# The first sequence of a gated attention kernel shares its scores between groups; the token sort works in two borrowed buffers

## The chip, the cores and the metric

The kernel runs on one core of a Trainium2 chip. The metric is the device time of one execution in microseconds (us), as the median of several runs. A profiled execution also gives a trace: every instruction with its start and its length, by engine. PE is TensorE (PEld its weight loads), DVE is VectorE, ACT is ScalarE, POOL is GpSimd, and SP is the engine whose queue issues most transfers.

## The reference

Two blocks follow each other. The first is gated attention over 8 sequences of 2496 tokens, without a softmax:

```
scores = z @ z^T / S            # z: (8, 2496, 64); each sequence's scores are symmetric
attn   = max(scores, 0) ** 2
x      = u * (attn @ v)         # u, v, x: (8, 2496, 256)
```

The second sends each of the 19968 tokens to one of 8 experts, by a hash of its id, and computes `max(x_e @ w1[e], 0) @ w2[e]` with w1 of 256 x 1024 and w2 of 1024 x 256. All in fp32.

## The kernel before, in words

**Tiling.** A sequence has 20 tiles of 128 tokens (T; the last holds 64), taken in five groups of four (G, NG). For a sequence b and a group g of queries, `scores` multiplies z with z on TensorE: one matmul gives a 128 x 512 block, tile t of the keys against the 512 queries of the group, into one of six PSUM buffers. A ReLU on the way to SBUF (L209 to L212) and a square in SBUF (`square`, L215) make it the attention weight. Four such blocks make a buffer `a`, of which there are seven (NA). `attend` then multiplies the weights with v, 4 matmuls per tile of keys, and accumulates in `acc`; `gate` multiplies with u and the constant.

**Sharing.** The block of keys t and queries s is the transpose of the block of keys s and queries t. From the second sequence on (`mirrored(b)`, L171) a group computes only the blocks of its own and of later groups (`fresh`), and VectorE transposes the blocks of a later group into a buffer `m` (`turns_of`, 16 instructions of 32 partitions x 512 for a 512 x 512 block), from which that later group reads them (`lhs`). Within a group's own 512 x 512 block part is skipped and transposed as well (`skipped`, `own_turns`; `fine(g)` is true for groups 2 to 4). The first sequence computes all 20 tiles in each group, its squares are on VectorE, and its ReLUs alternate between ScalarE and VectorE. In later sequences the squares are on ScalarE, and so are the ReLUs, but for every eighth one in groups 0 and 1.

**Order.** The order of all instructions on each engine is the program's, written out by hand. The loop over the 40 groups (L589) runs, for each group, in steps of four attention matmuls: a step squares two more tiles, calls `turn_scores(1)`, which puts out transposes worth 1600 elements of budget (a transposition of 512 elements is charged 682), and calls `between()`, which puts out one piece of other work. The next group's scores are put ahead of a group's last three tiles of attention, and the gates behind those. Transposes that must be done before a buffer is used again, or before a tile is read, are put out at once by `turn_now`.

**The other work.** In the first 40 steps, two groups long, `between` takes the next piece of `places()`, the token sort on VectorE (with six count matmuls on TensorE at L420), and at every fourth step `clear_x`, 2176 KB of zeros to the rows of x in DRAM. After that it puts out scatters on POOL: slots (`enter`) and rows of x (`place_x`). The sort keeps its arrays in a pool of its own, `route`, which is closed when the sort is done; the six turned buffers `m` are made after that, at the start of the fifth group.

**Loads.** SP's queue takes, in this order: z, v and u of the first sequence; at each group u of the next (two buffers: it waits for the gates two groups back); at a sequence's first group the z and v of the next (z has one buffer, v two); and the clears. The first z comes in a layout that TensorE transposes (L158); the later ones come in 12 transfers of runs of 128 bytes (L136 and L138) and are turned by VectorE in the fifth group (`turn_z`, L154).

Of the kernel before, what the change touches and what calls it, by code (L numbers as in the profile page):

```python
# [24 lines left out]
def kernel(  # L25
# [25 lines left out]
    G = 4  # L51
# [119 lines left out]
    def mirrored(b):  # L171
        return b > 0

    def fresh(b, g):

        if not mirrored(b):
            return [*range(T)]
        return [*range((g + 1) * G, T), *group(g)]

    def summed(b, g):  # L180

        own = group(g) if mirrored(b) else ()
        return [t for t in range(TM) if t not in own] + [t for t in own if t < TM]

    def skipped(b, g, t):

        if not mirrored(b) or t // G != g:
            return 0
        return (t % G if fine(g) else t % G // 2 * 2) * P

    def fine(g):

        return g > 1
# [3 lines left out]
    def scores(b, g):  # L197

        n = sum(width(t) for t in group(g))
        for k, t in enumerate(fresh(b, g)):  # L200
            lo = skipped(b, g, t)
            h = ds((t % 2 if t % G < 2 or not mirrored(b) else 1 - t % 2) * K, K)
            ps = mm_ps.tile([P, G * P], F32, name="s_ps", tag="mm")
            nc.tensor.matmul(ps[:, lo:n], zT[b][h, ts(t, P)], zT[b][h, ds(g * G * P + lo, n - lo)], start=True, stop=True)  # L204
            if t % G == 0:
                made[b, g, t // G] = apool.tile([P, G, G * P], F32, name="a", tag="a")
                rooms.append((b, g, t // G))
            a = made[b, g, t // G][:, t % G, lo:n]
            if (k % 8 == 7 and g < 2) if mirrored(b) else k % 2:  # L209
                nc.vector.tensor_scalar_max(a, ps[:, lo:n], 0.0)  # L210
            else:
                nc.scalar.activation(a, ps[:, lo:n], AF.Relu)  # L212
            to_square.append((b, g, t))

    def square(n):  # L215
        for b, g, t in to_square[:n]:
# [6 lines left out]
            for o, x in pairs:  # L223
                if mirrored(b):
                    nc.scalar.square(o, x)  # L225
                else:
                    nc.vector.tensor_mul(o, x, x)
            if mirrored(b) and t % G == G - 1:
# [46 lines left out]
    def turn_scores(steps):  # L275

        nonlocal turned
        turned += steps * 1600
# [94 lines left out]
    def places():  # L373

        with tc.tile_pool(name="route", bufs=1) as route:
# [16 lines left out]
            ones = route.tile([P, E * C], F32)  # L392
            nc.gpsimd.memset(ones[:], 1.0)

# [4 lines left out]
            for n, cols in ((P, slice(0, TM)), (R, slice(TM, T))):  # L399
# [4 lines left out]
            mask = route.tile([P, E, C], BF16)  # L404
            nc.vector.tensor_tensor(
                mask[:], eid[:].rearrange("p b t -> p (b t)").unsqueeze(1).to_broadcast([P, E, C]),
# [6 lines left out]
            total = route.tile([P, E, C], F32)  # L413
            rank = route.tile([P, E, C], F32)
# [8 lines left out]
            upto = route.tile([P, E, C], F32)  # L423
            flat = "p e c -> p (e c)"
            nc.vector.tensor_tensor_scan(upto[:].rearrange(flat), ones[:], total[:].rearrange(flat), 0.0,
                                         op0=OP.mult, op1=OP.add)
            yield
            nc.vector.tensor_add(rank[:], rank[:], upto[:])
            yield
            nc.vector.tensor_sub(rank[:], rank[:], total[:])  # L430
# [58 lines left out]
            nc.vector.tensor_add(rank[:], rank[:], shift[:].unsqueeze(2).to_broadcast([P, E, C]))  # L489
            yield  # L490
            nc.vector.tensor_mul(rank[:], rank[:], mask[:])
            yield
            slot = route.tile([P, C], F32)
            nc.vector.tensor_reduce(slot[:], rank[:].rearrange("p e c -> p c e"), axis=AX.X, op=OP.add)
# [91 lines left out]

    scores(0, 0)
    square(EARLY)
    for n, (b, g) in enumerate(groups):  # L589
        if n + 1 < len(groups):  # L590
            load_u(*groups[n + 1])
        if g == 0 and b + 1 < B:
            load_z(b + 1)
            load_v(b + 1)
        if n == NG - 1:
            m = pool("mirror", 1)
            mirrors = [m.tile([P, G, G, P], F32, name=f"m_{k}") for k in range(NG * NG // 4)]
# [171 lines left out]
```

## Time and profile before

The median of three runs is 2685.01 us (2684.61 to 2685.49). The profiled execution took 2687.06 us, with a span of 2685.1 us from its first to its last instruction, at a mean granted TensorE clock of 0.999.

| stretch, by the start of its first score matmul (us) | length | PE busy | DVE busy | ACT busy | DMA share |
|---|---|---|---|---|---|
| sequence 0, group 0: 13.79 to 53.93 | 40.14 | 38.72 | 30.22 | 6.55 | 1.01 |
| group 1: 53.93 to 96.58 | 42.65 | 42.65 | 28.95 | 5.97 | 1.02 |
| group 2: 96.58 to 139.24 | 42.66 | 42.66 | 21.10 | 5.97 | 0.29 |
| group 3: 139.24 to 181.89 | 42.65 | 42.65 | 20.60 | 5.97 | 0.08 |
| group 4: 181.89 to 221.03 | 39.14 | 39.14 | 23.52 | 5.80 | 0.09 |
| sequence 1, group 0: 221.03 to 262.55 | 41.52 | 41.20 | 31.42 | 18.43 | 0.48 |
| group 1: 262.55 to 303.05 | 40.50 | 40.50 | 34.01 | 14.60 | 0.09 |
| group 2: 303.05 to 341.63 | 38.58 | 38.58 | 33.15 | 10.89 | 0.09 |
| group 3: 341.63 to 378.49 | 36.86 | 36.86 | 30.74 | 6.86 | 0.09 |
| group 4: 378.49 to 411.04 | 32.55 | 32.55 | 23.93 | 3.05 | 0.11 |

A row is a stretch between the first score matmuls of two groups; since a group's scores stand ahead of the last three tiles of the group before, each stretch but the very first begins with one block of scores, ends the group before, and then attends. DMA share is the mean busy share of the 16 DMA engines. The other six sequences follow (the last score matmul starts at 1519.3 us), and the experts fill the rest. A line of a timeline gives start, us, engine, line of the kernel, operation, output and input, shapes and count; what stands in brackets at its end is how long the engine was idle before it and what ended that. Instructions that overlap on one engine are merged, so a line of 20 matmuls with 20 weight loads is x40.

### The profile page before, as it was taken

The page shows a single profiled execution, that of the slowest core. Times are in us where ns is not written, and L with a number is a line of the kernel's source. Part 1 is how long each engine was busy: PE and PEld are TensorE (multiplying, and loading weights), DVE is VectorE, ACT ScalarE, POOL GpSimd, SP SyncE. Part 2 cuts the span into 40 slices and gives each one's busy share as a digit, 9 for nine tenths or more (in the row PEclk, how much of TensorE's full clock was granted, in tenths as well). Part 3 has the DMA queues.
Part 4 walks back from the last instruction along what each step waited for, and adds up shares of the span by engine and source line. Part 5 has one row for each costly group of instructions (what it writes and reads, how often), then busy time and mean ns, then how long its engine had stood idle before and what let it go on. Part 6 is the DMA issues. An engine that isn't in the chain of part 4 may idle for free. (4 is left out here: it accounts for less than half of the span.)

```text
span 2685.1 us, 33980 instructions
## 1 busy us (share of the span) xinstructions
PE 2662.1 (99%) x12650; PEld 2255.2 (84%) x12650; DVE 1357.5 (51%) x2813; ACT 567.6 (21%) x1221; POOL 494.2 (18%) x513
## 2 busy tenths in 40 slices
PE   8999999999999999999999999999999999999998
PEld 6877887888888888888878888888888888888887
DVE  6556886887878878878878811111111111111110
ACT  2013314214222233123132111111111111111111
POOL 0221222122212221222101121111111111111113
PEclk9999999999999999999999999999999999999999
DMA  9612113013103122131101287777777777777773
GB/s 295 206 31 74 32 32 89 17 32 89 31 20 87 31 46 62 29 90 32 32 16 32 62 200 188 187 188 193 195 187 190 188 187 186 194 194 192 188 189 88
DMA packets 334842, 308.93 MB, mean 115 GB/s; under 512 B 187308, under 2 KB 293693, under 8 KB 334672
## 3 DMA queue, kind: packets, MB, share of 16 engines
q1 hardware_dynamic: 309424, 264.78, 39.2%
q0 software_dynamic: 21072, 41.10, 5.2%
q8 instruction: 102, 1.67, 0.3%
q10 hardware_dynamic: 4176, 0.82, 0.2%
q14 instruction: 68, 0.56, 0.1%
HBM read 243.25 MB, written 65.70 MB: 115 GB/s over the span
## 5 line engine op out<-in xcount | busy, mean ns | idle before, releaser
L329 PE MATMUL acc<-v_sb,a 128*128 128x256 f32 x3760 | 828.7, 380 | 3.7 <-issue 2.2
L329 PEld LDWEIGHTS acc<-v_sb,a 128*128 128x128 f32 x3760 | 710.3, 190 | 112.5 <-issue 7.9
L241 DVE STREAM_TRANSPOSE m<-a 32x512 f32<-32x512 f32 (+1 forms) x1120 | 756.8, 676 | 17.1 <-issue 0.3
L683 DVE TENSOR_SCALAR hT<-h_ps 128x512 f32<-128x512 f32 x162 | 112.1, 692 | 951.0 <-PE h_ps L675 933.9
L675 PE MATMUL h_ps<-v_sb,m 128*128 128x256 f32 x2592 | 586.0, 379 | 2.2 <-issue 1.1
L688 PE MATMUL o_ps<-m,hT 128*128 128x256 f32 x2592 | 585.2, 379 | 0.0
L675 PEld LDWEIGHTS h_ps<-v_sb,m 128*128 128x128 f32 x2592 | 492.3, 190 | 70.3 <-issue 2.1
L688 PEld LDWEIGHTS o_ps<-m,hT 128*128 128x128 f32 x2592 | 492.5, 190 | 67.0
L329 PE MATMUL acc<-v_sb,m 128*128 128x256 f32 x2016 | 439.7, 379 | 0.0
L329 PEld LDWEIGHTS acc<-v_sb,m 128*128 128x128 f32 x2016 | 383.0, 190 | 52.1
L212 ACT ACTIVATE a<-s_ps 128x512 f32<-128x512 f32 (+3 forms) x442 | 205.7, 578 | 902.9 <-PE s_ps L204 902.9
L522 POOL DMA_INDIRECT x_rows<-x_sb,slot_i x160 | 157.8, 986 | 1075.4 <-DVE x_sb L338 884.8
L700 POOL DMA_INDIRECT out_dram<-o_sb,idx x158 | 153.5, 972 | 918.7 <-ACT o_sb L695 903.8
L695 ACT COPY o_sb<-o_ps 128x256 f32<-128x256 f32 x162 | 60.3, 372 | 741.4 <-PE o_ps L688 737.5
L204 PE MATMUL s_ps<-zT 64*128 64x512 f32 (+5 forms) x1040 | 211.2, 549 | 0.0
L257 DVE STREAM_TRANSPOSE a<-a 32x128 f32<-32x128 f32 (+2 forms) x896 | 201.4, 249 | 7.8
L225 ACT ACTIVATE a<-a 128x512 f32<-128x512 f32 (+3 forms) x413 | 202.1, 625 | 0.0
L204 PEld LDWEIGHTS s_ps<-zT 64*128 64x128 f32 x1040 | 123.9, 187 | 81.8 <-issue 57.2
L510 POOL DMA_INDIRECT slot_tokens<-token,addr x160 | 158.8, 993 | 159.4 <-DVE addr L504 109.1
L681 ACT ACTIVATE hT<-h_ps 128x512 f32<-128x512 f32 x162 | 96.7, 597 | 229.0 <-PE h_ps L675 218.2
L210 DVE TENSOR_SCALAR a<-s_ps 128x512 f32<-128x512 f32 (+1 forms) x78 | 51.4, 659 | 146.6 <-PE s_ps L204 145.5
L338 DVE SCALAR_TENSOR_TENSOR x_sb<-acc,u_sb 128x256 f32<-128x256 f32 x152 | 57.9, 420 | 133.7 <-PE acc L329 132.8
(80 smaller groups left out, 380.6 us busy)
## 6 DMA issues: line engine op xcount, KB each, us to landing
m<-in_moe_w_dram SPq DMA_DIRECT2D x324, 256.0 KB
m<-in_moe_w_dram SPq DMA_DIRECT2D x81, 1024.0 KB
x_rows<-zero SPq DMA_DIRECT2D x10, 2176.0 KB
v_sb<-x_rows SPq DMA_DIRECT2D x324, 64.0 KB
v_sb<-in_v_dram SPq DMA_DIRECT2D x32, 512.0 KB
u_sb<-in_u_dram SPq DMA_DIRECT2D x32, 512.0 KB
zn<-in_z_dram SPq DMA_DIRECT2D x28, 304.0 KB
v_sb<-in_v_dram SPq DMA_DIRECT2D x8, 384.0 KB
```

Source lines behind the costliest of these rows:

```text
L204: nc.tensor.matmul(ps[:, lo:n], zT[b][h, ts(t, P)], zT[b][h, ds(g * G * P + lo, n - lo)], start=True, stop=True)
L212: nc.scalar.activation(a, ps[:, lo:n], AF.Relu)
L225: nc.scalar.square(o, x)
L241: nc.vector.transpose(mirror[b, a, g][ts(c, Q)].rearrange("p t s q -> p (t s) q")[:, 0:m, ts(r, Q)], made[b, a, g][ts(r, Q)].rearrange("p ...
L257: return n * Q, lambda: nc.vector.transpose(out, in_)
L329: nc.tensor.matmul(acc[i // 2][:, i % 2, :], lhs(b, g, t, i), v_sb[b][:, t, :], start=(k == 0 and i % 2 == 0), stop=(k == TM - 1), skip_gr ...
L510: st = nc.gpsimd.indirect_dma_start(out=slot_dram[:, None], out_offset=bass.IndirectOffsetOnAxis(ap=addr[0:n, c:c + 1], axis=0), in_=token ...
L522: st = nc.gpsimd.indirect_dma_start(out=x_dram[:, :], out_offset=bass.IndirectOffsetOnAxis(ap=slot_i[0:width(c % T), c:c + 1], axis=0), in ...
L675: nc.tensor.matmul(ps[:, i, :], w1[j][:, c, ts(f + i, P)], xT[j][:, :, c, :], start=(c == 0), stop=(c == DP - 1))
L683: nc.vector.tensor_scalar_max(o, ps[:], 0.0)
L688: nc.tensor.matmul(ps[:], hT[j][:, f, ts(t, P)], w2[j][:, f, :], start=(f == 0), stop=(f == FP - 1))
L700: st = nc.gpsimd.indirect_dma_start(out=out[:], out_offset=bass.IndirectOffsetOnAxis(ap=rows, axis=0), in_=o, in_offset=None, bounds_check ...
```

## The change

- `mirrored` is gone: the first sequence shares as the others do. Its groups 0 and 1 compute their own block in full (`skipped` is 0 there, and there are no `own_turns`); groups 2 to 4 skip and transpose as elsewhere. Group 0's scores come in the order of tiles 4 to 19, 0 to 3.
- All squares are on ScalarE. The ReLUs alternate between ScalarE and VectorE only in the first group of the first sequence. There the first two squares are put out after the eleventh score.
- The six turned buffers exist from the start. One of them, `sorting`, holds `upto` and `mask` of the sort until the third group begins, and joins the others then; `total` and `rank` lie in the z buffer, taken after the first z. `ones` shrinks to 8 columns and is broadcast in the long scan.
- The next sequence's z is loaded at group 2 instead of group 0, for all sequences.
- The budget of `turn_scores` is 1300 in the first 40 steps.

```diff
@@ -168,27 +168,23 @@
 
 
 
-    def mirrored(b):
-        return b > 0
-
     def fresh(b, g):
 
-        if not mirrored(b):
-            return [*range(T)]
         return [*range((g + 1) * G, T), *group(g)]
 
     def summed(b, g):
 
-        own = group(g) if mirrored(b) else ()
+        own = group(g)
         return [t for t in range(TM) if t not in own] + [t for t in own if t < TM]
 
     def skipped(b, g, t):
 
-        if not mirrored(b) or t // G != g:
+        if t // G != g or b == 0 and not fine(g):
             return 0
         return (t % G if fine(g) else t % G // 2 * 2) * P
 
     def fine(g):
+
 
         return g > 1
 
@@ -199,18 +195,20 @@
         n = sum(width(t) for t in group(g))
         for k, t in enumerate(fresh(b, g)):
             lo = skipped(b, g, t)
-            h = ds((t % 2 if t % G < 2 or not mirrored(b) else 1 - t % 2) * K, K)
+            h = ds((t % 2 if t % G < 2 else 1 - t % 2) * K, K)
             ps = mm_ps.tile([P, G * P], F32, name="s_ps", tag="mm")
             nc.tensor.matmul(ps[:, lo:n], zT[b][h, ts(t, P)], zT[b][h, ds(g * G * P + lo, n - lo)], start=True, stop=True)
             if t % G == 0:
                 made[b, g, t // G] = apool.tile([P, G, G * P], F32, name="a", tag="a")
                 rooms.append((b, g, t // G))
             a = made[b, g, t // G][:, t % G, lo:n]
-            if (k % 8 == 7 and g < 2) if mirrored(b) else k % 2:
+            if k % 2 if (b, g) == (0, 0) else k % 8 == 7 and g < 2:
                 nc.vector.tensor_scalar_max(a, ps[:, lo:n], 0.0)
             else:
                 nc.scalar.activation(a, ps[:, lo:n], AF.Relu)
             to_square.append((b, g, t))
+            if (b, g, k) == (0, 0, T // 2):
+                square(EARLY)
 
     def square(n):
         for b, g, t in to_square[:n]:
@@ -221,11 +219,8 @@
             if m < G * P:
                 pairs.append((short[0:width(t), t, :], a[0:width(t), ds(m, R)]))
             for o, x in pairs:
-                if mirrored(b):
-                    nc.scalar.square(o, x)
-                else:
-                    nc.vector.tensor_mul(o, x, x)
-            if mirrored(b) and t % G == G - 1:
+                nc.scalar.square(o, x)
+            if t % G == G - 1 and (t // G > g or b or fine(g)):
                 turns = turns_of(b, g, t // G) if t // G > g else own_turns(b, g)
                 to_turn.extend((n, (b, g, t // G), f) for n, f in turns)
 
@@ -275,7 +270,8 @@
     def turn_scores(steps):
 
         nonlocal turned
-        turned += steps * 1600
+
+        turned += steps * (1600 if i >= 2 * T else 1300)
         while to_turn and turned > 0:
             n, _, f = to_turn.pop(0)
             f()
@@ -389,8 +385,13 @@
             below = route.tile([P, P], BF16)
             nc.gpsimd.affine_select(out=below[:], in_=all1[:], pattern=[[1, P]], compare_op=OP.is_gt,
                                     fill=0.0, base=0, channel_multiplier=-1)
-            ones = route.tile([P, E * C], F32)
+            ones = route.tile([P, E], F32)
             nc.gpsimd.memset(ones[:], 1.0)
+            counts = npool.tile([P, 2, E, C], F32, name="zn")
+            total, rank = counts[:, 0], counts[:, 1]
+            room = sorting[:].rearrange("p t s q -> p (t s q)")
+            upto = room[:, 0:E * C].rearrange("p (e c) -> p e c", e=E)
+            mask = room[:, E * C:E * C + E * C // 2].bitcast(BF16).rearrange("p (e c) -> p e c", e=E)
 
 
             eid_i = route.tile([P, B, T], I32)
@@ -401,17 +402,14 @@
                 yield
                 nc.vector.tensor_copy(eid[0:n, :, cols], eid_i[0:n, :, cols])
                 yield
-            mask = route.tile([P, E, C], BF16)
             nc.vector.tensor_tensor(
-                mask[:], eid[:].rearrange("p b t -> p (b t)").unsqueeze(1).to_broadcast([P, E, C]),
+                mask, eid[:].rearrange("p b t -> p (b t)").unsqueeze(1).to_broadcast([P, E, C]),
                 iota_e[:].unsqueeze(2).to_broadcast([P, E, C]), op=OP.is_equal)
             yield
 
 
 
             yield
-            total = route.tile([P, E, C], F32)
-            rank = route.tile([P, E, C], F32)
             H = 512 // C
             for e in range(0, E, H):
                 m = min(H, E - e)
@@ -420,14 +418,13 @@
                     nc.tensor.matmul(ps[:, 0:m, :], w[:], mask[:, e:e + m, :], start=True, stop=True)
                     nc.vector.tensor_copy(dst[:, e:e + m, :], ps[:, 0:m, :])
                     yield
-            upto = route.tile([P, E, C], F32)
             flat = "p e c -> p (e c)"
-            nc.vector.tensor_tensor_scan(upto[:].rearrange(flat), ones[:], total[:].rearrange(flat), 0.0,
+            nc.vector.tensor_tensor_scan(upto.rearrange(flat), ones[:, 0:1].to_broadcast([P, E * C]), total.rearrange(flat), 0.0,
                                          op0=OP.mult, op1=OP.add)
             yield
-            nc.vector.tensor_add(rank[:], rank[:], upto[:])
-            yield
-            nc.vector.tensor_sub(rank[:], rank[:], total[:])
+            nc.vector.tensor_add(rank, rank, upto)
+            yield
+            nc.vector.tensor_sub(rank, rank, total)
             yield
 
 
@@ -486,12 +483,12 @@
             yield
 
 
-            nc.vector.tensor_add(rank[:], rank[:], shift[:].unsqueeze(2).to_broadcast([P, E, C]))
-            yield
-            nc.vector.tensor_mul(rank[:], rank[:], mask[:])
+            nc.vector.tensor_add(rank, rank, shift[:].unsqueeze(2).to_broadcast([P, E, C]))
+            yield
+            nc.vector.tensor_mul(rank, rank, mask)
             yield
             slot = route.tile([P, C], F32)
-            nc.vector.tensor_reduce(slot[:], rank[:].rearrange("p e c -> p c e"), axis=AX.X, op=OP.add)
+            nc.vector.tensor_reduce(slot[:], rank.rearrange("p e c -> p c e"), axis=AX.X, op=OP.add)
             yield
             nc.vector.tensor_copy(slot_i[:], slot[:])
             yield
@@ -584,17 +581,20 @@
         xT[j] = xT_buf[k]
         nc.vector.transpose(xT[j].rearrange("p k h i -> p (k h i)"), xg[j].rearrange("p k d -> p (k d)"))
 
+    mpool = pool("mirror", 1)
+    mirrors = [mpool.tile([P, G, G, P], F32, name=f"m_{k}") for k in range(NG * NG // 4)]
+
+    sorting = mirrors.pop()
     scores(0, 0)
-    square(EARLY)
     for n, (b, g) in enumerate(groups):
         if n + 1 < len(groups):
             load_u(*groups[n + 1])
         if g == 0 and b + 1 < B:
+            load_v(b + 1)
+        if g == 2 and b + 1 < B:
             load_z(b + 1)
-            load_v(b + 1)
-        if n == NG - 1:
-            m = pool("mirror", 1)
-            mirrors = [m.tile([P, G, G, P], F32, name=f"m_{k}") for k in range(NG * NG // 4)]
+        if n == 2:
+            mirrors.append(sorting)
 
         acc = [acc_ps.tile([P, 2, D], F32, name="acc", tag="acc") for _ in range(2)]
         for k in range(2):
```

## The prediction

> **What bounds the kernel now.** I read the page's busy shares first, then the waits of TensorE, then TensorE's and VectorE's timelines over the first two sequences.
>
> ```profile
> PE 2662.1 (99%) x12650; PEld 2255.2 (84%) x12650; DVE 1357.5 (51%) x2813; ACT 567.6 (21%) x1221; POOL 494.2 (18%) x513
> ```
>
> TensorE is busy for all but 23 of 2685.1 us at a granted clock of 0.999. Its waits (what waited for what: us in total, times, longest):
>
> ```profile
> PE z_ps L158 <- DMA zn<-in_z_dram: 9.4, 1, 9.4
> PE acc L329 <- issue: 2.2, 7, 0.3
> PE acc L329 <- DVE a L227: 1.4, 1, 1.4
> ```
>
> After the first z has landed nothing makes it wait for longer than 1.4 us. So a matmul taken away is time taken away, one for one, as long as no new wait appears; all the working below is TensorE's sum and a search for such waits.
>
> Its timeline (start, us, engine, line, what; each xN counts weight loads and matmuls, so x40 is 20 matmuls):
>
> ```profile
> 24.06 12.35 PE L329 MATMUL acc<-v_sb,a 128*128 128x256 f32 x56 [1.42 <-DVE a L227]
> ...
> 53.93 8.75 PE L204 MATMUL s_ps<-zT 64*128 64x512 f32 x40
> 62.61 33.07 PE L329 MATMUL acc<-v_sb,a 128*128 128x256 f32 x152
> ...
> 181.89 7.68 PE L204 MATMUL s_ps<-zT 64*128 64x448 f32 x40
> 189.50 26.17 PE L329 MATMUL acc<-v_sb,a 128*128 128x256 f32 x120
> ...
> 303.05 4.68 PE L204 MATMUL s_ps<-zT 64*128 64x512 f32 x24
> 307.66 5.45 PE L329 MATMUL acc<-v_sb,a 128*128 128x256 f32 x24
> ...
> 378.49 1.08 PE L204 MATMUL s_ps<-zT 64*128 64x448 f32 x8
> 379.50 5.45 PE L329 MATMUL acc<-v_sb,a 128*128 128x256 f32 x24
> ```
>
> From start to start: 20 score matmuls take 8.68 us (0.434 each), 7.61 in the last group. The second sequence, which already shares, spends 4.61 us in its group 2 and 1.01 in its group 4. The attention between two score blocks lasts 33.97 us in groups 1 to 3 of either sequence (62.61 to 96.58; 307.66 to 341.63).
>
> **Scores no longer computed (TensorE).** Group 0 keeps its 20 matmuls. Group 1 keeps 16 at full width (nothing is skipped in groups 0 and 1 of the first sequence): 8.68 - 16 x 0.434 = 1.74 saved. Groups 2, 3 and 4 become what they are in the second sequence: 8.68 - 4.61 = 4.07; 8.67 - 2.89 = 5.78 (139.24 to 147.91 against 341.63 to 344.52); 7.61 - 1.01 = 6.60. Sum **18.2 us**. The attention keeps its number of matmuls; reading a turned tile costs the same (32 matmuls in 13.8 us, 0.434 each, on either kind).
>
> **The first wait (TensorE, 1.42 us).** The first attention matmul waited for VectorE's square behind ten ReLUs. Now ScalarE squares the first two tiles in the middle of the score block (around 20 us), so it starts when the scores end, at 22.64. Gain **1.4**. The two squares put ScalarE about 1 us back; its ReLUs run 0.47 apart when fed (18 in 8.51 us) and are fed every 0.86 here, so it catches up within the last four, and PSUM's six buffers hide the rest. V's tiles 4 to 7, now read first, are in by then: at 229 to 367 GB/s from 5 us on, z, tokens and the first two V pieces are through before 15.
>
> **What VectorE gets.** It loses the first sequence's squares (100 tiles) and 38 of its 50 ReLUs, and gets the transposes of the shared tiles, between which the sort's steps stand. Its order in groups 0 and 1 is the point of the case:
>
> ```profile
> 23.32 2.49 DVE L227 TENSOR_TENSOR a<-a 128x512 f32<-128x512 f32 x4
> ...
> 46.57 2.81 DVE L425 TENSOR_TENSOR_SCAN upto<-ones,total 128x1280 f32<-128x1280 f32 x1
> ...
> 235.00 0.42 DVE L338 SCALAR_TENSOR_TENSOR x_sb<-acc,u_sb 128x256 f32<-128x256 f32 x1
> 235.46 11.46 DVE L241 STREAM_TRANSPOSE m<-a 32x512 f32<-32x512 f32 x16
> ```
>
> A transpose takes 11.46 / 16 = 0.716 us. The first can start when tile 7 is squared, at about 24.3 (ScalarE's last ReLU starts at 22.67, then two squares at 0.50). Before the ReLUs of group 1, 32 transposes stand in the queue (22.9 us) and the sort's steps up to the copy of `first`: eid 0.80, mask 1.48, six copies 3.62, scan 2.81, two adds 2.98, small 0.23: 11.9 us by their durations, 10.9 by their starts (a run of squares starts every 0.60 though each lasts 0.68: they overlap).
>
> Which of the two counts? [...] No row shows a sort step among transposes. [...] So VectorE comes to group 1's first ReLU at 24.3 + 22.9 + 12.5 = 59.7, done at 60.4. TensorE starts group 1's scores at 22.64 + 29.87 = 52.5 (29.87 is the old 24.06 to 53.93) and needs the PSUM buffer of score 7 for score 13, at 52.5 + 13 x 0.434 = 58.15. It waits **2.2 us**. By overlapped starts the ReLU would be done at 58.8 and the wait 0.7.
>
> The mask has to be there for the first count matmul at 34.8: 24.3 + ten transposes 7.2 + 0.8 + 1.5 + gaps = 33.9, in time by 0.9.
>
> **Group 1 and after.** TensorE ends the scores at 52.5 + 6.94 + 2.2 = 61.6 and group 0's last attention at 66.8 (12 matmuls), so group 0's last gates are done at 67.6. Behind them, ahead of group 1's gates, stand 36 transposes (28 x 0.716 + 8 of 32x384 at 0.58 = 24.7) and sort steps of 9.4 with 0.6 of gaps: VectorE is there at 102.3. TensorE starts group 2's scores at 61.6 + 33.97 = 95.6 and has data for the gates at 95.6 + 4.61 + 2.6 = 102.8. From there, eight transposes (5.7), the gates and three small steps (0.8), with the second pair of gates held to TensorE's 105.4, bring the tile shared by groups 1 and 2 to 111.2; TensorE asks for it at 105.4 + 16 x 0.434 = 112.4. No wait, by 1.2 us. Group 2 leaves VectorE over 4 us idle, and groups 3 and 4 are the second sequence's, where it keeps up (30.7 busy of 36.9 us, 23.9 of 32.6).
>
> ScalarE gets 60 squares at 0.50, two per 1.74 us of attention, and fewer ReLUs: hidden; uncovered it would be 30 us, over five groups of at least 32 us each.
>
> **The borrowed buffers.** `ones` becomes a broadcast column. A broadcast operand costs nothing beside a dense one in this trace (rank plus broadcast shift 1.47, rank plus upto 1.49), so the scan stays at 2.8; were it double, 2.8 us would come onto the wait at group 1. The z buffer is free once z is turned at 13.8, the first count is copied at about 37. GpSimd's smaller memset is long over either way. Five turned buffers suffice in groups 0 and 1 (four tiles of group 0, one of group 1); the sixth comes at group 2.
>
> **SP's queue.** The second z's 12 transfers leave the place between u(0,1) and v(1) (13.9 to 28.5, at 107 to 133 GB/s in the middle) and go behind u(0,3), which waits for group 1's gates, so at about 106. What moves up: v(1), the slot fill and the first five clears, some 15 us; V of the first sequence stands ahead of them. In the second sequence the 12 take from 235.83 to 248.3; so z lands by about 120 and is first turned some 12 us into group 4, at 183. Queued behind it is u(0,4), which waits for group 2's gates anyway, later. In later sequences z goes from 236 to about 314 with use at 390.75. All hidden; a late z would stall TensorE at once by what it is late. POOL's scatters only shift with the addresses, 112.9 to about 107.
>
> **Sum.** 18.2 + 1.4 - 2.2 = 17.4 from the profiled span of 2685.1, which lies 0.1 from the median of the runs: **2667.6**.
>
> **Rivals.**
> 1. No wait at group 1, or a mere trace: the sort's steps overlap or the squares are earlier. For it: the sort's first step, 0.24 long, lets the next square start after 0.15. Against: the gates beside transposes, which overlap nothing. 2685.0 - 19.6 + 0 to 0.7: 2665.4 to 2666.1.
> 2. Longer waits: the mask late, group 1's ReLU later by the scan or by slower small steps, then the 1.2 us margin in group 2 gone as well. 3 to 6 us more: 2670 to 2674.
> 3. Slower than before: transposes stretched while the DMA engines are full (share 1.01 and 1.02 in groups 0 and 1, where no transpose has run yet). 32 of them come ahead of group 1's wait and about 48 ahead of group 2's. All of 17.4 is lost when 80 x extra = 17.4 + 1.8 (the margins): 0.24 us each, 0.96 instead of 0.716. [...] Against it: of 1120 transposes none took over 0.709, those at full DMA (252 to 256, 413 GB/s) included, and squares start every 0.60 to 0.61 with full and with idle DMA.
> That the work isn't removed can be excluded: TensorE's program holds 40 score matmuls less.
>
> **How the numbers follow.** Forecast 0.58, rival 1 0.20, rival 2 0.17, rival 3 0.05. The bounds of the wait at group 1 are 0 and 5 us; 2665 to 2671.5 takes in rival 1 and the near part of rival 2. What a measurement can tell is about 0.2%, 5.4 us: all but rival 3 are faster by more; a little of rival 2's tail and of rival 3 falls within.
>
> **What would show it.** Score blocks of 6.9, 4.6, 2.9 and 1.0 us in groups 1 to 4; no wait ahead of the first attention matmul; one wait of s_ps on VectorE's ReLU of about 2 us near 58; the second sequence starting its scores near 203.6 instead of 221.0, and every later block shifted alike. It is wrong if waits of acc on m appear in groups 1 to 3, if a 32x512 transpose takes clearly over 0.71, or if z is turned late.

## The result, and the profile after

The changed kernel takes 2672.19 us (2671.7 to 2673.62, six runs) against 2684.91 us for the kernel before (2684.48 to 2685.49, six runs): a ratio of 0.9953, with a 95% interval of 0.994 to 0.9966. It is 12.7 us faster; 17.4 were forecast, and the time lies 0.7 us above the stated range. The profiled execution has a span of 2670.0 us.

The busy shares of the page, and the waits of TensorE (what waited for what: us in total, times, longest):

```profile
PE 2646.5 (99%) x12570; PEld 2250.0 (84%) x12570; DVE 1403.6 (53%) x2927; ACT 591.0 (22%) x1282; POOL 486.9 (18%) x513
```

```profile
PE z_ps L158 <- DMA zn<-in_z_dram: 9.3, 1, 9.3
PE acc L325 <- DVE x_sb L334: 2.2, 7, 0.3
PE s_ps L200 <- DVE a L206: 1.9, 1, 1.9
...
PE acc L325 <- DVE m L236: 0.8, 1, 0.8
```

The 40 score matmuls are gone: each fp32 score leaves two records on PE here (1040 records of scores have become 960), so 12650 has become 12570. (Ahead of the result a line's x40 was explained as 20 matmuls and 20 weight loads. The loads stand on PEld and are not in it; it is 20 matmuls of two records each. The six bf16 count matmuls leave six records.) The 1.42 us wait for VectorE's square is gone too. Two waits are new: the one foreseen, of the scores for a ReLU on VectorE, and one of 0.8 for a turned tile. TensorE's timeline over the first sequence:

```profile
22.89 12.35 PE L325 MATMUL acc<-v_sb,a 128*128 128x256 f32 x56
...
52.77 6.17 PE L200 MATMUL s_ps<-zT 64*128 64x512 f32 x26
60.85 2.38 PE L200 MATMUL s_ps<-zT 64*128 64x512 f32 x6 [1.91 <-DVE a L206]
63.16 6.69 PE L325 MATMUL acc<-v_sb,a 128*128 128x256 f32 x24
...
98.38 4.68 PE L200 MATMUL s_ps<-zT 64*128 64x512 f32 x24
102.98 5.45 PE L325 MATMUL acc<-v_sb,a 128*128 128x256 f32 x24
...
173.82 1.08 PE L200 MATMUL s_ps<-zT 64*128 64x448 f32 x8
174.83 5.45 PE L325 MATMUL acc<-v_sb,a 128*128 128x256 f32 x24
180.11 15.70 PE L325 MATMUL acc<-v_sb,m 128*128 128x256 f32 x72
196.65 5.45 PE L325 MATMUL acc<-v_sb,m 128*128 128x256 f32 x24 [0.84 <-DVE m L236]
```

Two lines beside the wait deserve a second look. The 12 attention matmuls at 63.16 last 6.69 us, while the same 12 at 102.98 last 5.45. And the 16 scores of group 1 end at 63.16, which is 10.4 us after they began, though 16 x 0.434 and the wait make only 8.9. The same stretch by windows (length; busy us and count of PE, PEld, DVE, ACT, POOL; granted clock; DMA share; GB/s) shows what happened:

```profile
58.00:60.00 2.00, 0.94 (x4) 0.11 (x1) 1.91 (x5) 1.32 (x3) 0.00 (x0) 1.00 0.00 1
60.00:62.00 2.00, 1.15 (x5) 0.68 (x6) 0.77 (x2) 0.60 (x1) 0.00 (x0) 1.00 0.01 4
62.00:64.00 2.00, 2.00 (x4) 0.75 (x4) 0.69 (x1) 1.33 (x3) 0.00 (x0) 0.57 0.00 0
64.00:66.00 2.00, 2.00 (x6) 1.61 (x6) 1.41 (x3) 2.00 (x5) 0.00 (x0) 0.57 0.00 0
```

TensorE's clock is halved from 62.3 to 65.7 us, 3.4 us in all, right behind the wait (the granted clock is 0.50 between 62.4 and 65.6). On VectorE the queue ahead of that ReLU looks as it was drawn up in the prediction (start, us, what):

```profile
26.12 0.24 DVE L401 TENSOR_SCALAR eid_i<-tok 128x152 int32<-128x152 int32 x1
26.39 1.42 DVE L236 STREAM_TRANSPOSE m<-a 32x512 f32<-32x512 f32 x2
...
48.87 2.83 DVE L422 TENSOR_TENSOR_SCAN m<-ones,zn 128x1280 f32<-128x1280 f32 x1
51.72 1.42 DVE L236 STREAM_TRANSPOSE m<-a 32x512 f32<-32x512 f32 x2
...
60.10 0.69 DVE L206 TENSOR_SCALAR a<-s_ps 128x512 f32<-128x512 f32 x1
```

Here a small step of the sort, put between transposes, holds the engine for its whole 0.24 us and 0.03 more (26.12 to 26.39); the ReLU starts at 60.10, where 59.7 was forecast.

### The profile page after: what moved, and what is told of

It is laid out like the page before. It is cut to its first block, busy times and chain, and to the rows that moved or that the text cites. A ratio compares the mean times of both kernels' runs of the same rounds, so it can differ in the third digit from the quotient of the medians.

```text
span 2670.0 us, 33997 instructions
## 1 busy us (share of the span) xinstructions
PE 2646.5 (99%) x12570; PEld 2250.0 (84%) x12570; DVE 1403.6 (53%) x2927; ACT 591.0 (22%) x1282; POOL 486.9 (18%) x513
## 5 line engine op out<-in xcount | busy, mean ns | idle before, releaser
L236 DVE STREAM_TRANSPOSE m<-a 32x512 f32<-32x512 f32 (+1 forms) x1280 | 865.0, 676 | 20.7 <-ACT a L222 0.9
L325 PE MATMUL acc<-v_sb,a 128*128 128x256 f32 x3472 | 768.3, 381 | 2.2 <-DVE x_sb L334 2.2
L325 PEld LDWEIGHTS acc<-v_sb,a 128*128 128x128 f32 x3472 | 656.5, 190 | 102.4 <-issue 6.9
L325 PE MATMUL acc<-v_sb,m 128*128 128x256 f32 x2304 | 502.8, 379 | 0.8 <-DVE m L236 0.8
L325 PEld LDWEIGHTS acc<-v_sb,m 128*128 128x128 f32 x2304 | 437.7, 190 | 60.7 <-DVE m L236 1.2
L208 ACT ACTIVATE a<-s_ps 128x512 f32<-128x512 f32 (+2 forms) x440 | 199.5, 574 | 867.2 <-PE s_ps L200 866.4
L222 ACT ACTIVATE a<-a 128x512 f32<-128x512 f32 (+3 forms) x472 | 231.8, 623 | 0.0
L252 DVE STREAM_TRANSPOSE a<-a 32x128 f32<-32x128 f32 (+1 forms) x992 | 220.6, 248 | 8.4
L200 PE MATMUL s_ps<-zT 64*128 64x512 f32 (+1 forms) x960 | 194.9, 545 | 1.9 <-DVE a L206 1.9
L206 DVE TENSOR_SCALAR a<-s_ps 128x512 f32<-128x512 f32 (+1 forms) x40 | 25.8, 645 | 91.4 <-PE s_ps L200 91.4
## 6 DMA issues: line engine op xcount, KB each, us to landing
x_rows<-zero SPq DMA_DIRECT2D x10, 2176.0 KB, 18.2
```

What stands on the lines that cost most here:

```text
L236: nc.vector.transpose(mirror[b, a, g][ts(c, Q)].rearrange("p t s q -> p (t s) q")[:, 0:m, ts(r, Q)], made[b, a, g][ts(r, Q)].rearrange("p ...
L252: return n * Q, lambda: nc.vector.transpose(out, in_)
L325: nc.tensor.matmul(acc[i // 2][:, i % 2, :], lhs(b, g, t, i), v_sb[b][:, t, :], start=(k == 0 and i % 2 == 0), stop=(k == TM - 1), skip_gr ...
```

## The experiments

The unit of all that follows is a group's stretch: from its first score matmul to that of the next group. They are read from TensorE's timeline, in us; the last column is the profiled span, and runs of one chip stand together.

| kernel | group 0 | 1 | 2 | 3 | 4 | span |
|---|---|---|---|---|---|---|
| the prediction's steps | 38.7 | 43.1 | 38.6 | 36.9 | 32.1 | |
| before | 40.14 | 42.65 | 42.66 | 42.65 | 38.72 | 2685.1 |
| changed | 39.01 | 45.61 | 38.58 | 36.86 | 33.22 | 2670.0 |
| *chip 5:* e1_relu | 38.65 | 41.14 | 42.87 | 36.86 | 33.22 | 2670.3 |
| e2_copies2 | 38.65 | 42.56 | 43.06 | 36.86 | 33.22 | 2673.3 |
| e3_budget | 39.24 | 45.60 | 41.96 | 36.87 | 32.11 | 2674.3 |
| e4_scan2 | 38.78 | 51.00 | 41.99 | 36.86 | 33.22 | 2680.7 |
| *chip 2:* after_again | 38.66 | 47.29 | 40.83 | 36.86 | 33.22 | 2673.9 |
| e7_z3 | 39.33 | 45.60 | 39.73 | 36.86 | 33.23 | 2672.5 |
| e8_best | 38.66 | 41.13 | 39.58 | 36.86 | 32.12 | 2665.6 |
| e9_zback | 38.84 | 45.59 | 42.51 | 36.86 | 33.23 | 2674.4 |
| *chip 13:* before_c | 40.68 | 42.65 | 42.66 | 42.65 | 38.72 | 2684.0 |
| before_again | 40.77 | 42.65 | 42.65 | 42.65 | 38.72 | 2683.8 |
| after_c | 38.66 | 47.29 | 38.58 | 36.86 | 33.22 | 2671.0 |
| after_d | 38.66 | 47.29 | 38.58 | 36.86 | 33.22 | 2670.9 |
| e11_first | 38.66 | 42.65 | 42.65 | 42.65 | 38.72 | 2681.2 |
| e10_late | 38.66 | 41.14 | 38.58 | 36.86 | 32.12 | 2663.7 |
| e10_c | 38.66 | 41.14 | 38.58 | 36.86 | 32.12 | 2664.1 |
| *chip 2 again:* before_e | 40.15 | 42.65 | 42.65 | 42.65 | 38.72 | 2684.8 |
| after_e | 38.65 | 47.29 | 41.87 | 36.86 | 33.22 | 2676.1 |
| e5_best | 38.66 | 41.14 | 41.40 | 36.86 | 32.12 | 2668.2 |

Group 4 of the kernel before is 38.72 here and not 39.14, as the table ahead of the prediction has it: the second sequence's first score starts at 220.61, between the last matmuls of the first, and not at 221.03.

```profile
220.61 0.69 PE L204 MATMUL s_ps<-zT 64*128 64x512 f32 x1
220.82 0.38 PE L321 MATMUL acc<-v_sb,a 64*128 64x256 f32 x1
221.03 4.45 PE L204 MATMUL s_ps<-zT 64*128 64x512 f32 x19
```

In the changed kernel that score starts at 207.04.

Group 0 varies by up to 0.7 with the moment at which the clock first comes up (at 12.2 to 15.3 us, around the start of its scores); the rest repeats to 0.03 us but for what the experiments are about, groups 1, 2 and 4. By the medians of several runs e1_relu takes 2671.81, e2_copies2 2674.57, e3_budget 2676.16 and e4_scan2 2681.77 us, with 2686.57 for the kernel before on chip 5; after_again 2675.39, e7_z3 2674.90 and e9_zback 2676.05, with 2686.44 on chip 2; after_c 2672.71, with 2685.07 on chip 13.

**The wait at group 1, taken away, shortened and lengthened.** Theory A: the wait costs more than it lasts, because the clock is halved behind it. Rival B: the half clock comes by itself. First, the two ReLUs on VectorE that the scores of group 1 wait for go to ScalarE:

```diff
-            if k % 2 if (b, g) == (0, 0) else k % 8 == 7 and g < 2:
+            if k % 2 if (b, g) == (0, 0) else k % 8 == 7 and g < 2 and b > 0:
```

> The changed kernel, with the two ReLUs of the first sequence's group 1 that VectorE does moved to ScalarE; nothing else. Theory A (the wait at group 1 costs more than it lasts, because TensorE's clock is halved after it): no wait of the scores on VectorE, no half clock near 62 us, the 16 scores in 7.0 us instead of 10.4; the profiled span goes from 2670.0 to about 2665.5 (1.9 of wait, 1.7 of half clock, 0.9 of score matmuls that run singly instead of in pairs). Rival B (the half clock has nothing to do with the wait): the half clock stays, near 62 us, and the span is 2667.2 to 2668.1.

Second, two of the six copies of counts go to ScalarE, so that VectorE is 1.4 us earlier:

```diff
-                    nc.vector.tensor_copy(dst[:, e:e + m, :], ps[:, 0:m, :])
+                    copy = nc.scalar.copy if e == 0 else nc.vector.tensor_copy
+                    copy(dst[:, e:e + m, :], ps[:, 0:m, :])
```

> The changed kernel, with the first two of the six copies of counts out of PSUM moved from VectorE to ScalarE. VectorE comes to group 1's first ReLU 1.4 us earlier, so the wait there is about 0.5 us instead of 1.9. Theory A with a length below which the clock stays up (the kernel before had 1.4 us without a drop): no half clock, span about 2666.5 to 2667. Rival (any wait at this place halves the clock): half clock for 3.4 us, span about 2668.5.

Third, the scan is done twice:

```diff
+            for _ in range(2):
-            nc.vector.tensor_tensor_scan(upto.rearrange(flat), ...
+                nc.vector.tensor_tensor_scan(upto.rearrange(flat), ...
```

> The changed kernel, with the long scan of the sort done twice, with the same result: 2.85 us more on VectorE ahead of group 1's first ReLU. The wait there grows from 1.9 to about 4.8 us. If time is lost only by the wait, the span is 2672.9. If a longer idle time also holds the clock down for longer (theory A, more than one period of 3.4 us at half), it is 2674 to 2675. The tile shared by groups 1 and 2 keeps its distance, since the gates are held to TensorE.

The score blocks of group 1 in these three, on TensorE's timeline; first without the VectorE ReLUs:

```profile
51.82 7.24 PE L200 MATMUL s_ps<-zT 64*128 64x512 f32 x32
...
92.96 4.68 PE L200 MATMUL s_ps<-zT 64*128 64x512 f32 x24
```

With two copies on ScalarE:

```profile
52.59 6.17 PE L200 MATMUL s_ps<-zT 64*128 64x512 f32 x26
59.27 1.98 PE L200 MATMUL s_ps<-zT 64*128 64x512 f32 x6 [0.50 <-DVE a L206]
```

With two scans:

```profile
52.59 6.17 PE L200 MATMUL s_ps<-zT 64*128 64x512 f32 x26
63.51 3.78 PE L200 MATMUL s_ps<-zT 64*128 64x512 f32 x6 [4.76 <-DVE a L206]
```

Each wait is as long as was expected. What it costs is group 1's stretch less the 41.14 of the kernel without it:

| kernel | wait | cost in group 1 | half clock behind it | cost less the wait and half of the half clock |
|---|---|---|---|---|
| e2_copies2 | 0.50 | 1.42 | none | 0.92 |
| changed, first profile; e3, e7, e9 | 1.9 | 4.47 | 3.4 us | 0.85 |
| after_again, after_c, after_d, after_e | 1.9 | 6.15 | 6.8 us | 0.83 |
| e4_scan2 | 4.76 | 9.86 | 10.2 us, 8.6 of it after the wait | 0.8 |

So theory A stands and B falls: without the wait the half clock near 62 us is gone, with a wait of half a microsecond there is none either, and behind a longer wait it lasts longer. The spans of e1_relu, e2_copies2 and e4_scan2 lie above what was expected (2670.3, 2673.3 and 2680.7), for the most part by the 4.3, 4.5 and 3.4 us that their group 2 loses; that loss has its own section below.

What is left, some 0.85 us whatever the wait, stands in the single records of the trace. The records of two scores (64*128 by 64x512) start together: in e1_relu the 32 records of the 16 scores make 16 starts, some 0.43 us apart. In the changed kernel the 13th score, the last before the wait, has no partner: its two records start alone, at 57.92 and 58.35. Behind the wait three scores are left: two starts in pairs, at 60.85 and 61.38, and two alone, at 61.81 and 62.24. That makes 18 starts instead of 16; the two more are 0.86 us.

**The wait in group 4.** Rival theories: transposes are put out too slowly in groups 2 to 4, or VectorE is full. VectorE's timeline of the changed kernel, at the gates of groups 2 and 3, and at the tile that was late:

```profile
142.74 0.76 DVE L334 SCALAR_TENSOR_TENSOR x_sb<-acc,u_sb 128x256 f32<-128x256 f32 x2 [4.94 <-PE acc L325]
...
177.72 0.76 DVE L334 SCALAR_TENSOR_TENSOR x_sb<-acc,u_sb 128x256 f32<-128x256 f32 x2 [3.33 <-PE acc L325]
...
195.44 1.16 DVE L236 STREAM_TRANSPOSE m<-a 32x384 f32<-32x384 f32 x2
```

It idles for 4.94 and 3.33 us in front of gates that are not ready, with transposes still to come; the last of the tile shared by groups 3 and 4 ends at 196.60, when TensorE has waited 0.84 us for it. The edit:

```diff
-        turned += steps * (1600 if i >= 2 * T else 1300)
+        turned += steps * (1300 if i < 2 * T else 1750 if i < 5 * T else 1600)
```

> The changed kernel, with the budget of transposes per step at 1750 instead of 1600 in groups 2 to 4 of the first sequence only. Theory: the 0.84 us wait for a turned tile in group 4 comes from transposes put out too slowly while VectorE idles before the gates (4.9 us in group 2, 3.3 in group 3), so it goes, and the second sequence starts 0.8 to 1.1 us earlier; the wait and the half clock at group 1 stay. Span 2668.9 to 2669.2. Rival (VectorE is simply full in the first sequence): the wait stays, or moves to the gates, and the span stays at 2670.0 or grows.

Group 4 falls from 33.22 to 32.11, and the wait for a turned tile is gone: as expected. The span is not: 2674.3 instead of about 2669, since 3.4 us were lost in group 2, where none of the four kernels had been expected to lose anything.

**Group 2: a loss that the first profile did not have.** In all four kernels on chip 5 group 2 took 42 to 43 us instead of 38.58. Was it the edits, or the chip? On chip 2 stood the changed kernel itself, and two edits of its loads, e7_z3 and e9_zback:

> The changed kernel itself, beside the next ones on one chip. Theory C (in group 2 of the first sequence TensorE runs out of instructions, because the transfer of its next block of them falls into the load of the second z, moved there by the change): either this profile shows it too, as waits of 2 to 2.6 us in all without a releaser some 14 us after the transfer, and a second half clock of 3.4 us, with a span of about 2674 to 2675; or this chip, like the first, has none in its profile, with about 2670.0. Rival (those waits came from the edits of the four kernels before): never here.

```diff
-        if g == 2 and b + 1 < B:
+        if g == (2 if b else 3) and b + 1 < B:
             load_z(b + 1)
```

> The changed kernel, with the second z loaded at group 3 of the first sequence instead of group 2 (later sequences as changed). The load then runs from about 146 to 160 us, between two transfers of TensorE's instructions (about 141 to 144 and 166), and z is first turned at about 186. Theory C: no waits without a releaser in groups 2 and 3 and no half clock there; span 2670.0 if the changed kernel shows none on this chip either, and some 4.2 us below it if it does. Rival (it is POOL's scatters, which begin in group 2, and not z): the waits stay in group 2.

```diff
-        if g == 2 and b + 1 < B:
+        if g == (0 if b else 2) and b + 1 < B:
             load_z(b + 1)
```

> The changed kernel, with the z of the third to eighth sequence loaded at group 0 as in the kernel before; the second z stays at group 2. The move of z costs nothing in later sequences where a transfer of instructions does not fall into it: same periods of 190.0 us between sequences as the changed kernel, the same span within 0.5 us. If loads at group 0 do meet such a transfer and that is what starves TensorE, waits without a releaser come up once per sequence, at up to 4 us each.

The changed kernel has a loss on chip 2 too (40.83), so the edits are not needed for it. With the second z at group 3 it takes 39.73, so half of the loss is gone; the other 1.15 us stays, and neither theory C nor its rival is right alone. (The medians of these two kernels are only 0.5 us apart, but e7_z3's profile and after_again's also differ by 1.7 us of half clock at group 1.) The z of later sequences makes no difference: sequences follow each other every 190.0 us in the kernel before, the changed one and e9_zback.

Does the kernel before lose there as well, on the same chip? Both kernels were profiled together on chip 13, where neither loses anything, and on chip 2:

> The kernel before, profiled beside the next ones: is there a wait without a releaser in its group 2 as well (96 to 140 us, where POOL's scatters begin) on a chip where the changed kernel has one? If the scatters alone starve TensorE of instructions, about 1 us of waits there. If it takes the change's load of z, none, and group 2 lasts 42.66 us as in the first profile.

> The kernel before on one chip with the next ones. If scatters alone starve TensorE on a chip where they do: group 2 (its first score to that of group 3) takes about 43.7 us instead of 42.65. If it takes the load of z in group 2: 42.65.

> The changed kernel. On a chip that starves: group 2 takes 40.8 to 42.9 us, the span is 2674 to 2675. On one that does not: 38.6 and 2670.

> The changed kernel once more: does the profile of the same kernel on the same chip differ in group 2 and in the length of the half clock after the wait at group 1 (3.4 or 6.8 us)? The wait itself, 1.9 us, is the same in each.

> The kernel before. On a chip that starves through scatters alone: about 43.7 us in group 2; otherwise 42.65.

> The changed kernel. On a chip that starves: 40.8 to 42.9 us in group 2 and a span of 2674 to 2675; otherwise 38.6, and 2670 to 2671 by the length of the half clock (3.4 or 6.8 us).

On chip 13 group 2 of the kernel before takes 42.65 in before_again and before_c, and that of the changed one 38.58 in after_c and after_d; both of the latter have 6.8 us of half clock behind the wait at group 1, where the first profile had 3.4. On chip 2 the kernel before takes 42.65, with its scatters in the same place, while the changed one takes 41.87. As far as one profile of the kernel before on chip 2 can tell, the loss in group 2 belongs to the change, on some chips. On TensorE's timeline of after_e it looks like this:

```profile
123.15 3.62 PE L325 MATMUL acc<-v_sb,a 128*128 128x256 f32 x16
126.97 0.38 PE L325 MATMUL acc<-v_sb,a 128*128 128x256 f32 x1 [0.20 <-issue]
128.41 0.38 PE L325 MATMUL acc<-v_sb,a 128*128 128x256 f32 x1 [1.07 <-issue]
129.83 0.38 PE L325 MATMUL acc<-v_sb,a 128*128 128x256 f32 x1 [1.05 <-issue]
130.54 9.87 PE L325 MATMUL acc<-v_sb,a 128*128 128x256 f32 x45 [0.33 <-issue]
```

For some 3.5 us matmuls trickle, with nothing that the profile shows them to wait for. In the eight profiles that lose time here with z loaded in group 2, it begins 13 to 15 us after a 16 KB transfer on a queue of instructions (at 113.6 us here), and within 2 us of the end of the second z's load (10240 packets of 128 bytes from 113.0 to 126.0 us here); in e7_z3 and e8_best, which load z later, 16 us after such a transfer. A half clock may follow (e1, e2 and e9, 3.4 us; not in after_e). Nor is the change alone in having such gaps: before and before_e have three or four of them near their end (0.14 to 0.63 us each, from 2663 to 2666), where no z is loaded, and no profile of chip 13 has them there. That TensorE runs short of instructions is a likely reading, not a shown one; what causes the 1.0 to 1.15 us that stay without the load of z, and why the same load costs nothing on chip 13 and in the first profile, is open.

**One part alone.** The kernel before, with nothing but the first two squares moved to ScalarE:

```diff
+            if (b, g, k) == (0, 0, T // 2):
+                square(EARLY)
-                if mirrored(b):
+                if mirrored(b) or (b, g) == (0, 0) and t < EARLY:
                     nc.scalar.square(o, x)
```

> The kernel before, with one part of the change alone: the first two squares of the first sequence go to ScalarE, in the middle of the first block of scores. The wait of 1.42 us ahead of the first attention matmul goes; everything after it is 1.4 us earlier and nothing else moves: 1.4 us less than the kernel before. If the squares hold ScalarE's ReLUs back, less than that, or a wait of the scores on ScalarE.

2683.45 us against 2685.31 (ratio 0.9994, interval 0.9984 to 1.0003): too small for the timing, but the trace has the step. The wait of 1.42 us for the square is gone from TensorE's waits, no wait of the scores on ScalarE takes its place, and group 0 lasts 38.66 us, as in those profiles of the changed kernel whose clock came up early.

**All together.** ReLUs on ScalarE, the budget of 1750, and the second z at group 3:

> All three edits on the changed kernel: group 1's two ReLUs on ScalarE, the budget of 1750 in groups 2 to 4, the second z at group 3. If the causes add: no wait of the scores, no half clock in the first sequence, no wait in group 4, no wait without a releaser; the second sequence's scores start at about 202.5 to 203.3 (206.3 with the ReLUs moved alone, less 4.2 for group 2, plus or minus the start, less 1.1 for group 4: 201.0 to 203.3), and the span is 2664.5 to 2666.5. If one cause only hides another, it stays above 2667.

The same with the second z left at group 2:

> The changed kernel with group 1's two ReLUs on ScalarE and the budget of 1750, the second z still at group 2. On a chip that starves: the same as with the ReLUs alone less 0.8 to 1.1, about 2669.3. On one that does not: 2664.0 to 2665, as good as with z at group 3.

And with POOL's scatters from group 3 on as well:

```diff
-        elif i % 4 == 0 and i < 2 * T + 4 * C:
-            for _ in place:
-                pass
-            enter((i - 2 * T) // 4)
+        elif i < 3 * T:
+            for _ in place:
+                pass
+        elif i % 4 == 0 and i < 3 * T + 4 * C:
+            enter((i - 3 * T) // 4)
```

> The kernel with all three edits (ReLUs on ScalarE, budget 1750, second z at group 3), and POOL's scatters begin at group 3 instead of group 2. If the 1.0 us that group 2 still lost without the load of z comes from the scatters, group 2 lasts 38.6 us instead of 39.6, and the span falls by 1.0 unless group 3, where both now meet, loses it instead: 2664.6. If TensorE runs short of instructions for a reason of its own, group 2 stays at 39.6.

> The kernel with the three edits and the scatters from group 3 on. If the load of z and the scatters are what starves TensorE there: 38.6 us in group 2 and no wait without a releaser in group 2 or 3 on any chip; span about 2663.7 to 2665, that is 19 to 21 us below the kernel before on the same chip. If group 3 now starves: 37.9 us or more there instead of 36.9.

e8_best takes 2667.74 us against 2686.44 on the same chip (ratio 0.9933, interval 0.9916 to 0.995), e5_best 2670.58 against 2686.88 (0.9943, 0.9926 to 0.9959), where group 2 loses 2.8 us, against 1.0 in e8_best. With late scatters, on chip 13, it is 2665.86 against 2685.31 (0.9929, 0.9911 to 0.9945) in e10_late and 2666.19 against 2685.07 (0.9929, 0.9911 to 0.9947) in e10_c, the same kernel again. That chip lost nothing in group 2 with the changed kernel either, so it does not tell what the late scatters are worth; it does show what the edits make of the rest. TensorE's waits in e10_c are down to the loads at the start and what the kernel before has too:

```profile
PE z_ps L158 <- DMA zn<-in_z_dram: 9.5, 1, 9.5
PE acc L325 <- DVE x_sb L334: 2.2, 7, 0.3
PE h_ps L676 <- ACTq L731: 1.2, 1, 1.2
```

From before_c to e10_c the second sequence's first score comes 20.05 us earlier (221.24 to 201.19), of which 0.05 is the start and some 0.5 the clock's coming up during group 0. The rest, 19.5, is close to the prediction's 18.2 + 1.4, with no wait to take off.

## Why the prediction was wrong

**The scores no longer computed: right.** 18.2 us were forecast; groups 2 and 3 came out at 38.58 and 36.86 as worked out, and groups 1 and 4 do so where the new waits are removed (41.14 and 32.12, against 40.9 and 32.1).

**The first wait: right.** It is gone, in the changed kernel and with that part alone. Of the 1.42 us, 0.3 were lost in the first profile to a clock that came up 0.8 us later than in the profile before.

**VectorE's queue and the length of the wait: right.** The 2.2 us rest on 12.5 us for the sort's steps ahead of the ReLU, their whole durations (11.9) and 0.6 of gaps. No run on record before the result shows that term; to count whole durations and not starts was the author's choice. In the changed kernel 35.43 us pass from the first transpose to that ReLU (24.67 to 60.10): 22.5 of the 32 transposes, 11.9 of the sort's steps and 1.0 between them, where 35.4 were forecast. The wait is 1.91 in eight profiles. Overlapped starts would have given 0.7.

**The price of the wait: wrong.** The prediction's step "It waits **2.2 us**" put 2.2 into the sum. The wait cost 4.5 us in the first profile and 6.2 in others: 1.9 of standing still, 0.85 for the two scores that lost their partner, and 1.7 or 3.4 us because the clock was halved for 3.4 or 6.8 us. This one term holds 2.3 to 4.0 of what is missing. "One for one, as long as no new wait appears" had to go on: and no wait behind which the clock drops.

After how much idle time did it drop? In the first profile the half clock lasts 3.41 us, and the clock drops 47.8 us after it came up, which is 14 times 3.41; the half clocks of the other profiles last one, two or three times 3.41. So take the traces of all 20 profiles, from the moment when the clock comes up to the last matmul, in windows of 3.41 us, and add up the time between matmuls in each. At full clock, eleven windows idle for 1.72 us or more (1.72 in e1_relu to 3.12 in e4_scan2), and the clock drops behind each; it drops behind none that idles for up to 1.48. Of the two windows between, with 1.64 (e7_z3) and 1.68 (after_e), it drops behind the first. So in these traces the drop came with about half a window of idle time or more, as near as the modelled ends of matmuls allow. The first profile of the kernel before, with its wait of 1.42 us, has no window with more than 1.36 and keeps its clock, and so does e2_copies2 behind its wait of 0.5; after_e's four gaps in group 2, 2.65 us in all, lie in two windows, with 1.68 and 0.97, and the clock stays up.

What decides between 3.4 and 6.8 us is not shown. In the four profiles with 6.8 the first window behind the drop still holds 2.2 to 2.7 us of scores; in the four with 3.4 it holds 0.3 to 1.2.

**Group 4: wrong, by an unworked margin.** For groups 1 and 2 the prediction worked out when each turned tile is ready; for groups 3 and 4 it said that they "are the second sequence's, where it keeps up". They are for TensorE, not for VectorE: by the ends of groups 0 to 3 the first sequence has started 27, 68, 102 and 136 transposes into turned buffers, the second 34, 74, 109 and 144. So it enters group 4 with 24 still to do instead of 16. It falls behind in group 0, where the budget is 1300 and the sort stands among the transposes (which of the two counts for more was not tried), and the steps after that put them out at the usual pace while the engine idled. The prediction's signs of being wrong named a wait for a turned tile in groups 1 to 3 only. Price 1.1 us, 0.84 of it the wait.

**SP's queue: wrong on some chips.** The second z lands in time, as said, and never holds up what needs it. "All hidden" missed that its load can cost TensorE time in another way: on chip 2 group 2 loses 2.2 to 3.9 us with the load in it (four profiles, one of them with a half clock behind the loss), and 1.0 and 1.15 with the load at group 3. In the first profile there is nothing of it.

The sum for the first profile, from the start of the first score to the second sequence's: 18.2 of scores, plus 1.1 of the first wait, less 4.5 of the wait at group 1 and 1.1 at group 4, less 0.2 by which group 1 stays above the forecast even without its wait (41.14 against 40.9; in e1_relu ScalarE's ReLUs start every 0.48 us, and the scores every 0.43): 13.5. Measured: 206.8 to 193.3 us, 13.5. The two profiled spans differ by 15.1, which flatters the change: from its last score to its last matmul the profile before took 1.5 us longer (1158.1 against 1156.6), with 1.2 us of gaps from 2663 to 2666 that the profile after does not have, and with 2687.06 us it lay 2.05 above the median of its runs. The prediction set its sum against the span and, though it gave that time, did not ask what of the span was particular to this execution; as a difference the sum is not touched by it. The profile after was a cheap one, too: three of the six runs of the changed kernel have spans of 2670.0 to 2670.2, the others 2670.8 to 2671.9, as after_c and after_d have with the longer half clock (2671.0 and 2670.9). That the slower three had it as well is likely; they were not profiled.

**The second rival: its range, not its causes.** The time lies in the range of the second rival, 2670 to 2674, but that is luck. Nothing waited for the mask, the wait at group 1 was shorter than forecast and not longer, and the tile shared by groups 1 and 2 was in time.

## What to carry to other kernels

A wait of TensorE is not priced by its length alone. Here 1.9 us of standing still cost 4.5 to 6.2, with a half clock behind them, and half a microsecond only 1.4, without one, so when a change to a full TensorE makes one wait, look in the trace for the clock behind it, and ask first whether the wait can be shortened: two ReLUs moved to a less busy engine took 4.5 us out of that group. Look at its neighbours as well: this wait split 16 paired scores into 13 and 3, and the odd one of each ran alone, at some 0.85 us in all.

A queue that was nearly full in one stage hands its backlog on. Follow each late item to its own deadline in every later stage, and look where the engine idles in front of something that is not ready while work with a deadline stands behind it.

## What the runs showed of the hardware

- TensorE's clock stayed at half, and between two changes at full, for multiples of 3.41 us (3.41 and 47.8 in the first profile of the changed kernel). Cut into windows of that length, the 20 profiles have twelve behind which it dropped to half, with 1.64 (e7_z3) to 3.12 us (e4_scan2) between matmuls, and it dropped behind none with up to 1.48; behind one with 1.68 (after_e) it did not. The half clock lasted 3.4 us in the first profile of the changed kernel and 6.8 in after_again, after_c, after_d and after_e, with the same wait of 1.9; in e4_scan2, with a wait of 4.8 us, 10.2.
- The scores (64*128 by 64x512) start in pairs, some 0.43 us apart (e1_relu); one without a partner takes two such starts (57.92 and 58.35 in the first profile of the changed kernel). A wait behind an odd score cost 0.83 to 0.92 us in this way, beside its length and the clock.
- In the changed kernel a VectorE step of 0.24 us between two transposes of 32 partitions holds the engine for 0.25 to 0.27 us (26.12 to 26.39); ahead of a square, in the kernel before, the same step lets it start after 0.15 (25.73 to 25.88).
- On chip 2 a load of 10240 packets of 128 bytes, beside POOL's scatters, was followed by some 3.5 us in which matmuls started one by one without waiting for anything that the profile knows (after_e, group 2 41.87 us); on chip 13 the same kernel ran through (after_c, 38.58).
